# Attention and GLU block on one core: products beside the scores as column tiles, chord additions mostly on GpSimd, chunks of 256 queries, one running-sum bank

## The chip, the cores and the metric

One core of a Trainium2 chip runs the kernel. The metric is the device time of a run in microseconds (us), and lower is better. A run counts as slow when it is over 1.5% above the fastest of its kernel. A page is the profiler's summary of one execution, the span runs from its first to its last instruction, and the granted clock is the share of its full speed that TensorE was allowed. Engine names in the profile are PE (TensorE matrix products), PEld (TensorE weight loads), DVE (VectorE), ACT (ScalarE), POOL (GpSimd) and SP (SyncE, here only transfers).

## The reference, cut to what matters

The input has 2048 rows of 640. There are 32 query heads of size 20, which share one key and one value head. A GELU-gated MLP of width 1536 follows.

```python
def _A_ref(x, wq, wk, wv, wo):
    q = (x @ wq).reshape(B, S, 32, 20).transpose(0, 2, 1, 3)
    k = x @ wk
    v = x @ wv
    scores = jnp.einsum("bhqd,bkd->bhqk", q, k) * (20 ** -0.5)
    p = _softmax(scores, axis=-1)
    o = jnp.einsum("bhqk,bkd->bhqd", p, v)
    return o.transpose(0, 2, 1, 3).reshape(B, S, 640) @ wo

h = x + _A_ref(_layernorm(x), ...)
h2 = h + down(gelu(g) * u)        # g, u: products of layernorm(h) with w_gate, w_up
```

The 32 x 2048 x 2048 exponentials dominate. They are 2048 tiles of 128 keys x 512 columns.

## The kernel before

A score product fills four PSUM banks, one for each 32-row tile of the array. Each bank is a tile of 128x512 scores. ScalarE turns a tile (or two at once) into exponentials in `pa`. VectorE does the same for other tiles by integer arithmetic: it scales a score to the bit pattern of a bf16 power of two, which is a chord of the exponential. Two more copies with 42 and 85 added to the bits give two other chords. The three are summed with different weights in the value product, so a VectorE tile costs one pass over PSUM, two additions in SBUF and three value products instead of one.

```python
CH_SHIFT = (0, 42, 85)
...
# VectorE: the first chord, from PSUM to SBUF as uint16
op = plan.commit("dve", lambda e: e.tensor_scalar(pd[:, 0, s * 512:(s + 1) * 512], bank(b), CH_A, CH_B,
                                                  ALU.mult, ALU.add), c_dve(512), L_DVE, ...)
...
def do_adds(t):                    # VectorE: the other two chords, up to 4 tiles at once
    ...
    for w in (1, 2):
        a = slice(s0 * 512, (s0 + k) * 512)
        op = plan.commit("dve", (lambda w, a: lambda e: e.tensor_scalar(
            pd[:, w, a], pd[:, 0, a], float(CH_SHIFT[w]), None, ALU.add))(w, a), k * 512 / 3.84 + 60.0, L_DVE, ...)
...
# value products: four column tiles of 32, one for each head row
ins = e.matmul(ps[32 * r:32 * r + 32, ab * 512:(ab + 1) * 512], v_ext[:, it["kt"], it["w"], :],
               it["ap"], start=st, stop=(j in ends), tile_position=(0, 32 * r))
```

Every instruction goes through `plan.commit` with an assumed cost in ns. A list scheduler runs once while the program is built. With those costs it fixes the order on each engine, the buffers, and which engine gets which score tile. On the chip the order never changes.

The softmax here doesn't subtract the row's maximum and nothing guards it: scores larger than these inputs give would overflow.

Of the kernel before, what the change touches and what calls it, by code (L numbers as in the profile page):

```python
# [191 lines left out]
def bass_sequential_preLN__grouped_kv_mqa__glu_gated_geglu__prompt_kernel(  # L192
# [30 lines left out]
    CHUNKS = [[0], [1], [2, 3], [4, 5, 6, 7], [8, 9, 10, 11], [12, 13], [14], [15]]  # L223
    BATCHES = [[0, 1, 2, 3], [4, 5, 6, 7], [8, 9, 10, 11], [12, 13], [14], [15]]
    BATCH_COL = [0, 0, 0, 0, 256, 384]
# [65 lines left out]
    def c_mm(n):  # L291
        return max(n / 2.4, 54.0) + 3.0
# [6 lines left out]

    L_PE, L_ACT, L_DVE, L_POOL = 250.0, 165.0, 150.0, 100.0  # L300
# [47 lines left out]
    state = {"mode": "m", "tab": "exp", "npack": 0, "exps_left": 2048, "kv_left": NT, "qk_left": 512}  # L348
# [27 lines left out]
    def ln_group(ln, tiles, prio, done):  # L376
# [27 lines left out]
        def norm(t):  # L404
# [9 lines left out]
            def then(op):  # L414
                s = slot[0]

                def tdone(op2):
                    slots["xt"].append(s)
                    done(t, op2)

                if ln == 0:
                    o = xn1T[:, :, t * P:(t + 1) * P]
                    wkeys = [("xn1T", t)]
                else:
                    o = xn2T[:, :, xcol[t]:xcol[t] + P]
                    wkeys = [("xn2T", xcol[t])]
                sp_tasks.append(_Task(("sp",), lambda e: e.dma_start_transpose(o, xn_tmp[:, s, :]), 1330, 1500,
                                      [("xt", s)], wkeys, prio, tdone))
# [15 lines left out]

    xcol = {}
# [8 lines left out]
    def mm(o, l, r, st, sp, **kw):  # L454
        return lambda e, b: e.matmul(o(b), l, r, start=st, stop=sp, **kw)  # L455
# [95 lines left out]
    def on_job(u, so):  # L551
# [8 lines left out]
        def then(b):  # L560
# [4 lines left out]
            def c1(op):  # L565
# [3 lines left out]
                if nt == 4:  # L569
                    g = gs[0]  # L570
                    o = onq[:, tl[0] % NON:tl[0] % NON + 4, 4 * Dh * g:4 * Dh * (g + 1)].rearrange(
                        "p j (r d) -> p j r d", r=4)
                    parts.append((o, slice(0, 4)))
                elif nt == 2:
                    for gi, g in enumerate(gs):
                        o = onq[:, tl[0] % NON:tl[0] % NON + 2, 4 * Dh * g:4 * Dh * (g + 1)].rearrange(
                            "p j (r d) -> p j r d", r=4)
                        parts.append((o, slice(2 * gi, 2 * gi + 2)))
                else:
                    o = onq[:, tl[0] % NON, 4 * Dh * gs[0]:4 * Dh * (gs[-1] + 1)].rearrange(  # L580
# [10 lines left out]
                for o, js in parts:  # L591
# [4 lines left out]
                        [("onq", t % NON, g) for t in tl for g in (gs if nj == 4 else [gs[js.start // 2]])],  # L596
# [5 lines left out]
        def gate():  # L602
            return bool(slots["rcp"])
# [11 lines left out]
    def on_transpose(t):  # L615
        sl = []
        tk = _Task(("sp",), None, 1330, 1500, [("onq", t % NON, g) for g in range(NG)], [], 1.0, None,
                   lambda: bool(slots["onT"]))

        def bind():  # L620
            s = slots["onT"].pop(0)
            sl.append(s)
            tk.fn = lambda e: e.dma_start_transpose(onT[:, s, :, :], onq[:, t % NON, :])
            tk.writes = [("onT", s)]
# [26 lines left out]
    LN2G = [[0], [1], [2, 3], [4, 5], [6, 7], [8, 9], [10, 11], [12, 13], [14], [15]]  # L651
# [15 lines left out]
    def x2_done(t, op):  # L667
        b = batch_of[t]
        batch_x[b] += 1
        if batch_x[b] == len(BATCHES[b]):  # L670
            for fc in range(NFC):
                gate_job(b, fc)
# [9 lines left out]
    def g_free(b):  # L682

        if b <= 3:
            return all(down_left[x] == 0 for x in range(b))
        return all(down_left[x] == 0 for x in range(min(b, 3)))

    def gu_pieces(w, b, fc):
        n = len(BATCHES[b]) * P
        x0 = xcol[BATCHES[b][0]]  # L690
        return [(mm(lambda bk: bank(bk, n), w[:, c, fc * P:(fc + 1) * P], xn2T[:, c, x0:x0 + n],
                    c == 0, c == NC_D - 1), c_mm(n),
                 [("xn2T", xcol[t]) for t in BATCHES[b]] + ["wg" if w is wg_sb else "wu"]) for c in range(NC_D)]

    def gate_job(b, fc):
        n = len(BATCHES[b]) * P

        def then(bk):
            def fin(op):
                free_bank(bk)  # L700
                gate_left[b] -= 1
# [4 lines left out]
            def fin2(op):  # L706
                free_bank(bk)
                gate_left[b] -= 1
# [3 lines left out]
            o = gbuf[:, fc, gcols(b)]  # L712
            if state["exps_left"] > 0:
                dve(lambda e: e.tensor_copy(o, bank(bk, n)), c_dve(n), [("b", bk)], gkeys(b, fc), 1.0, fin)
            else:
                task(("act",), lambda e: e.activation(o, bank(bk, n), ACT.Gelu_apprx_tanh), ("gelu", c_act(n)), L_ACT,  # L716
                     [("b", bk)], gkeys(b, fc), 1.0, fin2)
        jobs.append(_Job(("gate", b, fc), 5.0, gu_pieces(wg_sb, b, fc), then, lambda: g_free(b)))

    def gelu(b):  # L720
        fcs = sorted(copied[b])
        runs = []
        for fc in fcs:
            if runs and runs[-1][1] == fc and fc - runs[-1][0] < 3:
                runs[-1][1] = fc + 1
            else:
                runs.append([fc, fc + 1])
        n = len(BATCHES[b]) * P
        for f0, f1 in runs:
            v = gbuf[:, f0:f1, gcols(b)]  # L730
            ks = [k for fc in range(f0, f1) for k in gkeys(b, fc)]
            task(("act",), (lambda v: lambda e: e.activation(v, v, ACT.Gelu_apprx_tanh))(v),  # L732
                 ("gelu", c_act(n * (f1 - f0))), L_ACT, ks, ks, 1.0,
                 (lambda f0, f1: lambda op: [up_job(b, fc) for fc in range(f0, f1)])(f0, f1))

    def up_job(b, fc):
        n = len(BATCHES[b]) * P

        def then(bk):
            def fin(op):  # L740
                free_bank(bk)
                up_left[b] -= 1
# [3 lines left out]
            o = gbuf[:, fc, gcols(b)]  # L746
            dve(lambda e: e.tensor_tensor(o, bank(bk, n), o, ALU.mult), c_dve(n), [("b", bk)] + gkeys(b, fc),  # L747
                gkeys(b, fc), 1.0, fin)
# [46 lines left out]


    act_q = []
    dve_q = []
    pend = []
    groups = [(0, 1), (2, 3), (4, 5)]  # L800
# [26 lines left out]
    def free_groups(t):  # L827
        res = []
        for a, b in groups:
            if bank_owner[a] is None and bank_owner[b] is None:  # L830
                r = plan.ready("pe", (), [("b", a), ("b", b)])
                res.append((r, a, b))
        res.sort()
        return [g for g in res if g[0] <= t + 30], res
# [7 lines left out]
    def dve_load(t):  # L842
        v = max(plan.free["dve"] - t, 0.0)
        v += sum(600.0 for x in dve_q) + 300.0 * (len(pend) + len(dve_q))
        m = sum(tk.cost if isinstance(tk.cost, float) or isinstance(tk.cost, int) else 0.0
                for tk in tasks if tk.engs[0] == "dve")
        return v + min(m, 1500.0)

    def issue_qk(t, u, kt, gs):
# [5 lines left out]
        best = None  # L855
        for n, ca in ((0, 1810.0), (1, 1382.0), (2, 904.0), (3, 478.0), (4, 0.0)):
            if n > nf or (n and state["npack"] < 4):
                continue
            m = max(A + ca, Dv + 900.0 * n)
            if best is None or m < best[0] - 1.0:  # L860
                best = (m, n)
        n = best[1]
        (_, a0, a1), (_, b0, b1) = gs[0], gs[1]
# [5 lines left out]
        if n <= 2:  # L869
            lay = [(rr[2], a0), (rr[3], a1), (rr[0], b0), (rr[1], b1)]  # L870
        else:
            lay = [(rr[0], a0), (rr[1], a1), (rr[2], b0), (rr[3], b1)]
# [10 lines left out]
        sw = 0.0 if state["mode"] == "q" else SW  # L883
# [6 lines left out]
        if n == 0:  # L890
            act_q.append(("P", [tiles[rr[0]], tiles[rr[1]]]))
            act_q.append(("P", [tiles[rr[2]], tiles[rr[3]]]))
        elif n == 1:
            dve_q.append(tiles[rr[0]])
            act_q.append(("S", [tiles[rr[1]]]))
            act_q.append(("P", [tiles[rr[2]], tiles[rr[3]]]))
        elif n == 2:
            dve_q.append(tiles[rr[0]])
            dve_q.append(tiles[rr[1]])
            act_q.append(("P", [tiles[rr[2]], tiles[rr[3]]]))  # L900
        else:
            for i in range(n):
                dve_q.append(tiles[rr[i]])
            if n == 3:
                act_q.append(("S", [tiles[rr[3]]]))
# [6 lines left out]
        state["npack"] += 1  # L912
        state["qk_left"] -= 1
# [3 lines left out]
    def acc_bank(u):  # L917
        if u["acc"] is None:
            for b in (6, 7):
# [21 lines left out]
    def issue_pv(t, qs, k):  # L941
# [29 lines left out]
        sw = 0.0 if state["mode"] == "v" else SW  # L971
        state["mode"] = "v"
        op = plan.commit("pe", fn, 216.0 * k + sw, L_PE, reads, writes, at=t)
# [37 lines left out]
    def pe_decide(t):  # L1011
        cand = next_pack(t)
        ok, allg = free_groups(t)
        if cand and len(ok) >= 2:
# [4 lines left out]
        if cand:  # L1019
            est = [g[0] for g in allg]  # L1020
            ta = plan.free["act"]
            fin = {}
            for kind, tl in act_q:
                ta = max(ta, tl[0]["vis"]) + c_act(512 * len(tl))
                for x in tl:
                    fin[x["b"]] = ta + L_ACT
            td = plan.free["dve"]
            for x in dve_q:
                td = max(td, x["vis"]) + 600
                fin[x["b"]] = td + L_DVE  # L1030
            have = set((g[1], g[2]) for g in allg)
            for a, b in groups:
                if (a, b) not in have:
                    e1 = fin.get(a, None)
                    e2 = fin.get(b, None)
                    ra = plan.ready("pe", (), [("b", a), ("b", b)])
                    if (e1 is None and bank_owner[a] is not None) or (e2 is None and bank_owner[b] is not None):
                        est.append(1e12)
                    else:
                        est.append(max(e1 or 0, e2 or 0, ra))  # L1040
            est.sort()
            tq = est[1]
# [6 lines left out]
        press = pa_free.count(True) < 5 or (pd_free.count(True) < 3)  # L1049
        if press and nr == 0:  # L1050
            nr = min(most, 1)
        piece = next_piece(t)

# [3 lines left out]
        def do_pv():  # L1057
            sw = 0.0 if state["mode"] == "v" else SW
            k = int((lim - t - sw) // 216.0) if lim < 1e11 else 3
            k = max(1, min(k, nr, 4))  # L1060
# [8 lines left out]
        swv = 0.0 if state["mode"] == "v" else SW  # L1069
        swm = 0.0 if state["mode"] == "m" else SW  # L1070
        can_v = nr >= 1 and (fits(216.0 + swv) or press)
# [375 lines left out]
```

## Time and profile before

The median is 849.52 us. The profiled run has a span of 851.3 us.

| what (before) | number | where |
|---|---|---|
| ScalarE busy | 763.4 us, 90% | page, part 1 |
| VectorE busy | 742.2 us, 87% | page, part 1 |
| GpSimd busy | 26.9 us, 3% | page, part 1 |
| attention | 24.5 to 792 us | first and last exponential on ScalarE |
| tail | 59.5 us | span less the start of the last exponential (791.8 us) |

First come two parts of the page of the kernel before: busy time by engine with the share of the span and the instruction count, and the shares of the chain that ended last.

```profile
PE 730.3 (86%) x6973; PEld 269.4 (32%) x6973; DVE 742.2 (87%) x1856; ACT 763.4 (90%) x1070; POOL 26.9 (3%) x60
...
ACT 66%; PE 20%; DVE 10%; DMA 3%; issue 1%; SPq 0%; DVEq 0%
```

Next, the costliest groups of the same page. The columns are: line, engine, operation, output from input, shapes and count | busy us, mean ns of one | idle time before, and what ended it. A group whose line says "+1 forms" mixes shapes in its mean.

```profile
L1212 ACT ACTIVATE pa<-ps 128x512 bf16<-128x512 f32 (+1 forms) x1006 | 722.1, 935 | 21.4 <-PE ps L880 20.7
L1263 DVE TENSOR_SCALAR pd<-ps 128x512 uint16<-128x512 f32 x520 | 355.2, 687 | 48.4 <-PE ps L880 40.7
...
L1245 DVE TENSOR_SCALAR pd<-pd 128x512 uint16<-128x512 uint16 (+2 forms) x832 | 230.2, 319 | 8.8
```

Then two windows from the middle of the attention. The columns after the stretch and its length are busy us and instruction count of PE, PEld, DVE, ACT and POOL, then the granted clock, the DMA share and GB/s.

```profile
200.00:400.00 200.00, 176.90 (x1615) 53.99 (x1611) 183.25 (x439) 195.86 (x269) 0.70 (x1) 0.95 0.02 5
400.00:600.00 200.00, 182.25 (x1685) 58.20 (x1683) 187.65 (x450) 198.04 (x274) 1.41 (x2) 0.98 0.06 11
```

ScalarE is 98 to 99% busy there, VectorE 92 to 94%, and GpSimd stands idle. That is why the additions look like work to give away: 230 us of VectorE time.

Only a few GpSimd instructions exist in this kernel. The following are three of its groups with the shapes kept apart, and below them two single instructions of one line (count: duration in ns as min/median/max, first and last start).

```profile
L491 POOL TENSOR_SCALAR v_ext<-v_ext 128x40 bf16<-128x40 bf16 x14 | 4.9, 348 | 22.1 <-DVE v_ext L505 15.5 <-DVE ln_r L397 4.0 <-DVE ln_veb L389 2.0
L332 POOL COPY wq_pad<-gbuf 128x400 bf16<-128x400 bf16 x8 | 3.8, 520 | 4.3 <-DMA gbuf<-in_A_wq_dram 4.3
...
L491 POOL TENSOR_SCALAR v_ext<-v_ext 128x20 bf16<-128x20 bf16 x4 | 1.3, 327 | 0.9 <-ACT v_ext L504 0.7
...
L491 POOL TENSOR_SCALAR v_ext<-v_ext x1: 258/258/258, 25.0 to 25.0; 128x20 bf16<-128x20 bf16 x1
L491 POOL TENSOR_SCALAR v_ext<-v_ext x1: 308/308/308, 29.4 to 29.4; 128x40 bf16<-128x40 bf16 x1
```

A copy of 400 elements takes 0.52 us. The scalar operation that the change wants to send there is present only with 20 and 40 elements.

### The profile page before, as it was taken

What the parts mean: (1) busy time and instruction counts of PE and PEld (TensorE: products, weight loads), DVE (VectorE), ACT (ScalarE), POOL (GpSimd) and SP (SyncE); (2) the same over time, 40 slices, a digit from 0 to 9 for tenths busy, and PEclk for the clock granted to TensorE, in tenths of its full rate; (3) what the DMA queues carried; (4) which work ended last, traced back from release to release, by engine and by line L of the source; (5) the groups of instructions that cost most, each with busy time, mean ns of one, the idle gap of its engine ahead of it and who ended that gap; (6) DMA issues with size and microseconds to landing.
All of it is one profiled execution on the core that took longest, in us unless ns stands there. A gap on an engine that the chain in (4) does not pass through costs nothing.

```text
span 851.3 us, 17702 instructions
## 1 busy us (share of the span) xinstructions
PE 730.3 (86%) x6973; PEld 269.4 (32%) x6973; DVE 742.2 (87%) x1856; ACT 763.4 (90%) x1070; POOL 26.9 (3%) x60
## 2 busy tenths in 40 slices
PE   0877778778889989999998998999999999898998
PEld 0522222222222222233332222223333333232587
DVE  7768988987898989999999998999999999899533
ACT  0779999999999999999999999999999999999322
POOL 5300000000000000000000000000000000000000
PEclk9969979996898999999999998999999999999999
DMA  6780000100000000000021000000102000000100
GB/s 180 144 283 1 16 2 9 10 1 1 7 12 16 1 2 1 2 1 8 27 31 32 2 1 1 2 1 2 39 2 55 2 2 17 17 9 9 32 17 33
DMA packets 42930, 21.84 MB, mean 26 GB/s; under 512 B 34016, under 2 KB 41568, under 8 KB 42848
## 3 DMA queue, kind: packets, MB, share of 16 engines
q1 hardware_dynamic: 40224, 19.83, 9.6%
q8 instruction: 57, 0.93, 0.5%
q10 hardware_dynamic: 2624, 0.87, 0.5%
q14 instruction: 25, 0.20, 0.1%
HBM read 10.21 MB, written 2.62 MB: 15 GB/s over the span
## 4 chain that ended last, share of the span: by engine, by line
ACT 66%; PE 20%; DVE 10%; DMA 3%; issue 1%; SPq 0%; DVEq 0%
ACT pa L1212 64%; PE ps L455 11%; PE ps L968 5%; PE ps L880 5%; DVE pd L1263 4%; DVE pd L1245 2%; ACT gbuf L732 1%; DMA xn1T<-xn_tmp 1%; DMA xh<-in_A_x_dram 1%; DVE stats L374 1%; DVE stats L367 1%; DMA onT<-onq 0%; DVE xn_tmp L435 0%; DVE xh L646 0%; ACT L1212 0%
## 5 line engine op out<-in xcount | busy, mean ns | idle before, releaser
L1212 ACT ACTIVATE pa<-ps 128x512 bf16<-128x512 f32 (+1 forms) x1006 | 722.1, 935 | 21.4 <-PE ps L880 20.7
L1263 DVE TENSOR_SCALAR pd<-ps 128x512 uint16<-128x512 f32 x520 | 355.2, 687 | 48.4 <-PE ps L880 40.7
L968 PE MATMUL ps<-pd,v_ext 128*32 128x512 bf16 x1560 | 280.3, 405 | 21.3 <-ACT pa L1212 14.1
L968 PE MATMUL ps<-pa,v_ext 128*32 128x512 bf16 x1528 | 272.2, 404 | 11.8 <-ACT pa L1212 8.0
L880 PE MATMUL ps<-qT,kT 32*128 32x512 bf16 x2048 | 211.4, 401 | 53.9 <-ACT pa L1212 26.0
L1245 DVE TENSOR_SCALAR pd<-pd 128x512 uint16<-128x512 uint16 (+2 forms) x832 | 230.2, 319 | 8.8
L880 PEld LDWEIGHTS ps<-qT,kT 32*128 32x128 bf16 x2048 | 57.9, 91 | 229.5 <-DVE pd L1263 195.1
L968 PEld LDWEIGHTS ps<-pd,v_ext 128*32 128x32 bf16 x1560 | 67.2, 95 | 110.1 <-issue 47.9
L968 PEld LDWEIGHTS ps<-pa,v_ext 128*32 128x32 bf16 x1528 | 66.1, 94 | 92.4 <-issue 42.0
L455 PE MATMUL ps<-xn2T,wu_sb 128*128 128x512 bf16 (+2 forms) x360 | 69.0, 317 | 6.0 <-DVE gbuf L747 5.9
L455 PE MATMUL ps<-xn2T,wg_sb 128*128 128x512 bf16 (+2 forms) x360 | 68.1, 311 | 0.0
L455 PE MATMUL ps<-xn1T,wq_pad 128*128 128x128 bf16 (+2 forms) x320 | 47.9, 288 | 21.1 <-DMA xn1T<-xn_tmp 20.3
L455 PE MATMUL ps<-wd_sb,gbuf 128*128 128x320 bf16 x384 | 59.6, 300 | 0.0
L747 DVE TENSOR_TENSOR gbuf<-ps,gbuf 128x512 bf16<-128x512 f32 (+2 forms) x72 | 36.5, 509 | 18.3 <-PE ps L455 11.9
L716 ACT ACTIVATE gbuf<-ps 128x128 bf16<-128x128 f32 (+1 forms) x36 | 11.2, 312 | 38.1 <-PE ps L455 38.1
L455 PEld LDWEIGHTS ps<-wd_sb,gbuf 128*128 128x128 bf16 x384 | 34.3, 98 | 20.9 <-issue 8.1
L455 PEld LDWEIGHTS ps<-xn2T,wu_sb 128*128 128x128 bf16 x360 | 26.6, 99 | 32.3 <-issue 14.3
L393 POOL TENSOR_TENSOR ln_denb<-ln_veb,halfc 128x2 bf16<-128x2 bf16 (+1 forms) x19 | 12.6, 673 | 749.1 <-DVE ln_veb L389 749.1
L455 PEld LDWEIGHTS ps<-xn1T,wq_pad 128*128 128x128 bf16 x320 | 23.2, 103 | 39.8 <-DMA xn1T<-xn_tmp 20.3
L455 PEld LDWEIGHTS ps<-xn2T,wg_sb 128*128 128x128 bf16 x360 | 25.8, 98 | 25.1 <-issue 14.7
L766 DVE TENSOR_TENSOR xh<-xh,ps 128x320 bf16<-128x320 bf16 x32 | 15.4, 482 | 17.4 <-PE ps L455 17.4
L455 PE MATMUL ps<-wo_sb,onT 128*128 128x320 bf16 x160 | 28.3, 301 | 0.1
(47 smaller groups left out, 266.2 us busy)
## 6 DMA issues: line engine op xcount, KB each, us to landing
out_dram<-xh SPq DMA_DIRECT2D x16, 160.0 KB, 1.8
xh<-in_A_x_dram SPq DMA_DIRECT2D x3, 640.0 KB, 9.9
wg_sb<-in_B_w_gate_dram SPq DMA_DIRECT2D x1, 1920.0 KB, 8.9
wu_sb<-in_B_w_up_dram SPq DMA_DIRECT2D x1, 1920.0 KB, 10.2
wd_sb<-in_B_w_down_dram SPq DMA_DIRECT2D x1, 1920.0 KB, 14.0
gbuf<-in_A_wq_dram ACTq DMA_DIRECT2D x2, 400.0 KB, 8.3
wo_sb<-in_A_wo_dram SPq DMA_DIRECT2D x1, 800.0 KB, 5.3
xh<-in_A_x_dram SPq DMA_DIRECT2D x2, 160.0 KB, 2.8
```

The source lines that it names most:

```text
L367: dve(lambda e: e.bn_stats(stats[:, ln, t, 6:12], xh[:, t, HALF:D]), 356, [key], [("st", ln, t, 1)], prio, c)
L374: dve(lambda e: e.bn_stats(stats[:, ln, t, 0:6], xh[:, t, 0:HALF]), 356, [key], [("st", ln, t, 0)], prio, b)
L393: task(("pool",), lambda e: e.tensor_tensor(ln_denb[:, ln, sl], ln_veb[:, ln, sl], halfc[:, 0:n], ALU.pow), 1010, L_POOL, [("veb", kk), "h ...
L455: return lambda e, b: e.matmul(o(b), l, r, start=st, stop=sp, **kw)
L716: task(("act",), lambda e: e.activation(o, bank(bk, n), ACT.Gelu_apprx_tanh), ("gelu", c_act(n)), L_ACT, [("b", bk)], gkeys(b, fc), 1.0, fin2)
L747: dve(lambda e: e.tensor_tensor(o, bank(bk, n), o, ALU.mult), c_dve(n), [("b", bk)] + gkeys(b, fc), gkeys(b, fc), 1.0, fin)
L766: dve(lambda e: e.tensor_tensor(xh[:, t, h * HALF:(h + 1) * HALF], xh[:, t, h * HALF:(h + 1) * HALF], bank(bk, HALF), ALU.add), c_dve(HALF ...
L880: ins = e.matmul(bank(b), kT4[32 * r:32 * r + 32, kt * P:(kt + 1) * P], qT[32 * r:32 * r + 32, s, :], start=True, stop=True, tile_position ...
L968: ins = e.matmul(ps[32 * r:32 * r + 32, ab * 512:(ab + 1) * 512], v_ext[:, it["kt"], it["w"], :], it["ap"], start=st, stop=(j in ends), ti ...
L1212: op = plan.commit("act", lambda e: e.activation(dst, src, ACT.Exp, scale=SM_SCALE), cost, L_ACT, [("b", b0 + i) for i in range(n)], [("pa ...
L1245: op = plan.commit("dve", (lambda w, a: lambda e: e.tensor_scalar(pd[:, w, a], pd[:, 0, a], float(CH_SHIFT[w]), None, ALU.add))(w, a), k * ...
L1263: op = plan.commit("dve", lambda e: e.tensor_scalar(pd[:, 0, s * 512:(s + 1) * 512], bank(b), CH_A, CH_B, ALU.mult, ALU.add), c_dve(512), ...
```

## The change

The intent: GpSimd takes most of the additions, so VectorE can take more score tiles from ScalarE. TensorE changes between only two tilings, because all products beside the scores are split in four column tiles like the value products. Chunks of at most 256 queries let the MLP of early rows run inside the attention. With one bank for the running sum, other banks can hold scores. Gate and up products fill a whole bank before they are evicted. The core of the diff (the plumbing of buffers and of the scheduler's choices is left out):

```diff
-    CHUNKS = [[0], [1], [2, 3], [4, 5, 6, 7], [8, 9, 10, 11], [12, 13], [14], [15]]
-    BATCHES = [[0, 1, 2, 3], [4, 5, 6, 7], [8, 9, 10, 11], [12, 13], [14], [15]]
+    CHUNKS = [[0, 1], [2, 3], [4, 5], [6, 7], [8, 9], [10, 11], [12, 13], [14], [15]]
+    BATCHES = CHUNKS
...
+    POOL_ADD = 520.0
+    ADD_MIN = 2
...
+        def fn(e, b, mode):
+            if mode == "m":
+                return e.matmul(o(b), l, r, start=st, stop=sp)
+            ins = None
+            for j in range(4):
+                a = slice(32 * j, 32 * j + 32)
+                ins = e.matmul(o(b)[a, :], l[:, a], r, start=st, stop=sp, tile_position=(0, 32 * j))
+            return ins
...
     def acc_bank(u):
         if u["acc"] is None:
+            if state["kv_left"] == 0 and any(bank_owner[b] is not None and bank_owner[b][0] == "acc" for b in (6, 7)):
+                return False
...
+        a = slice(s0 * 512, (s0 + k) * 512)
+        cost, lat = (k * 512 / 3.84 + 72.0, L_DVE) if eng == "dve" else (POOL_ADD, L_POOL)
+        op = plan.commit(eng, lambda e: e.tensor_scalar(pd[:, w, a], pd[:, 0, a], float(CH_SHIFT[w]), None, ALU.add),
+                         cost, lat, ...)
...
     def pool_decide(t):
...
+        if POOL_ADD:
+            w = 2 if len(pend[2]) >= len(pend[1]) else 1
+            if pend[w] and pend[w][0]["at"] <= t + 20:
+                do_adds(t, "pool", w, 1)
```

The instruction orders of the two programs, which can be compared without a run, show 1146 additions on GpSimd and 119 instructions of addition left on VectorE. VectorE takes 648 score tiles instead of 520. TensorE changes its tiling 1023 times instead of 1272.

## The prediction

> **What bounds the kernel now.** From 24 to 792 us the attention runs, then a tail of about 58 us. The chain of waits gives 64% of the span to the exponentials on ScalarE. The windows of 100 us between 200 and 700 us show ScalarE 98 to 100% busy, VectorE 91 to 96%, TensorE 86 to 92% (its record includes pipeline ends). The groups: 522 pair exponentials (128x1024) and 484 single ones on ScalarE, busy 722.1 us; on VectorE 520 exponentials from the score banks (355.2 us) and 832 chord additions (230.2 us). So ScalarE binds, VectorE is close behind, GpSimd is idle (3%).
>
> **What the change moves** (counts from the two instruction orders):
> 1. VectorE takes 648 of 2048 score tiles, not 520. ScalarE has 389 pairs and 622 singles. In the timeline a pair takes 0.914 us start to start and a single 0.475; both kernels so computed, times 1.02 (what the old sum lacks to 722), give 722 before and 664 after. Six more table loads (1.283 us each) and slightly more GELU work return 10 us. ScalarE: about 48 us less in the attention.
> 2. VectorE loses 713 additions (119 remain, about 38 us; minus 190) and gains 128 tiles (0.60 to 0.65 us start to start; plus 80). Busy falls from 742 to about 635 us.
> 3. GpSimd gets 1146 additions of 128x512 uint16. The case has no such instruction: small GpSimd scalar operations (20 to 40 elements) take 0.26 to 0.31 us, copies of 400 elements come 0.46 us apart. The Trainium skill (GPSIMD Engine Reference, section 3.1) gives 1.03 cycles per element for such bodies, 0.44 us for 512 as an estimate; with overhead I expect 0.52 to 0.7 us, so 600 to 800 us in all. No run here shows it yet. At 0.52 it fits; at 0.65 GpSimd binds beside ScalarE. The same page says (section 8) that contention comes with VectorE's two-port modes or two SBUF inputs; few of those are left, so I expect little.
> 4. TensorE: mode changes fall from 1272 to 1023. The Trainium skill (TensorEngine Tiling, Key Properties) says that a change of mode drains; the timeline agrees, about 0.11 us lost each, so 28 us saved. But four column tiles instead of one instruction nearly double the instructions, small products (128 columns) get slower (estimate 99 instead of 57 ns per group), 256 queries mean more groups, and value products rise from 3088 to 3344 (18 us). Net: TensorE work about 15 to 20 us more, none of it on the path while ScalarE binds.
> 5. Tail: after the last score product some 277 column groups remain (about 28 us), then one tile's projection, norm and GLU (about 28 us): as long as now.
>
> **Sum.** Only the attention shortens: 48 us if ScalarE stays the limit with the same idle time, giving 802. I give back 13 us for idling, as four engines now run at 80 to 95% in a fixed order with one sum bank and freer score banks. Predicted: **815 us**, range 792 to 866 (8 in 10). Faster by over 2%: 0.69; within 2%: 0.16; slower by over 2%: 0.15.
>
> **What would show it.** ScalarE exponentials 655 to 670 us busy and still 94% or more of the attention; VectorE additions below 45 us; GpSimd 600 to 700 us busy with TensorE rarely waiting for its additions; the last exponential ends near 755 us; tail 53 to 60 us.
>
> **What would make it wrong.** A GpSimd addition over 0.65 us: value products then wait for GpSimd, buffers of the VectorE tiles stay full, and the time goes to 850 us or beyond. Column tiles limited by weight loads would make TensorE the limit. Planned order not matching real durations would leave ScalarE idle.

## The result, and the profile after

The changed kernel takes 1776.68 us (median of 2 runs), against 849.52 us. The ratio is 2.091, with a 95% interval of 2.082 to 2.100. Every ratio in this document is the mean time of one kernel's fast runs over that of the other's in the same rounds, so it is not quite the ratio of the medians. The prediction was 815 us, and even its range ended at 866.

The same parts of the page after:

```profile
PE 996.2 (56%) x13866; PEld 385.8 (22%) x13866; DVE 679.3 (38%) x1268; ACT 757.0 (43%) x1055; POOL 1697.3 (96%) x1205
...
POOL 93%; issue 3%; DMA 1%; PE 1%; DVE 1%; SPq 0%; POOLq 0%
```

GpSimd went from 3 to 96% busy and holds 93% of the chain; ScalarE and VectorE stand idle more than half of the time. The groups of the page after:

```profile
L1329 POOL TENSOR_SCALAR pd<-pd 128x512 uint16<-128x512 uint16 x1146 | 1671.6, 1488 | 3.0 <-DVE ln_vb L399 2.2
L1296 ACT ACTIVATE pa<-ps 128x512 bf16<-128x512 f32 (+1 forms) x1011 | 712.6, 762 | 939.3 <-PE ps L988 802.9
L1350 DVE TENSOR_SCALAR pd<-ps 128x512 uint16<-128x512 f32 x648 | 432.2, 687 | 931.4 <-PE ps L988 927.7
L1067 PE MATMUL ps<-pa,v_ext 128*32 128x512 bf16 x1400 | 381.7, 515 | 448.3 <-POOL pd L1329 447.7
```

One addition on GpSimd takes 1.488 us, not 0.52, and GpSimd waited only 3.0 us before all 1146 of them: it never had nothing to do. The sum is the whole time. The first addition starts at 35.7 us. 1146 of them keep GpSimd busy for 1671.6 us, about 11 us go to norms, small copies and idling between them, and the last one starts at 1716.7 us and ends near 1718. With the 35.7 us before the first addition and the 56 us after the last, that is the span of 1774.5 us.

The waits of the same run (engine, line, what it waited for: us in total, times, longest) show how the delay is handed on:

```profile
DVE pd L1350 <- PE ps L988: 927.7, 354, 8.5
PEld ps L1067 <- POOL pd L1329: 834.1, 393, 7.9
ACT pa L1296 <- PE ps L988: 802.9, 348, 10.6
PE ps L1067 <- POOL pd L1329: 697.6, 351, 7.6
```

TensorE waits for GpSimd in the value products (the second and fourth line). The order of its work is fixed, so the next score product stands behind that wait, and ScalarE and VectorE wait for the score product. A stretch of the timeline (start us, us, engine, line, operation, and in brackets the idle time before it) shows one such wait:

```profile
803.96 4.39 POOL L1329 TENSOR_SCALAR pd<-pd 128x512 uint16<-128x512 uint16 x3
...
804.41 0.57 PE L1067 MATMUL ps<-pa,v_ext 128*32 128x512 bf16 x1
804.41 0.57 PE L1067 MATMUL ps<-pd,v_ext 128*32 128x512 bf16 x2
...
806.95 0.39 PE L1067 MATMUL ps<-pd,v_ext 128*32 128x512 bf16 x1 [1.97 <-POOL pd L1329]
```

The three additions take 4.39 us, and between 804.98 and 806.95 us TensorE does nothing.

The granted TensorE clock is 0.70 after and 0.96 before, and a matrix product takes 0.515 us instead of 0.404. The column tiles are not the reason: the second experiment has them too, and its clock is 0.96. The lower clock came together with a TensorE that was idle for 44% of the span; what sets it was not tested. It is not what made the run long either, since GpSimd waited for others for only 3.0 us before its additions.

### The profile page after: what moved, and what is told of

Read it like the earlier page. It is cut to its first block, busy times and chain, and to the rows that moved or that the text cites. A ratio compares the mean times of both kernels' runs of the same rounds, so it can differ in the third digit from the quotient of the medians.

```text
span 1774.5 us, 32037 instructions
## 1 busy us (share of the span) xinstructions
PE 996.2 (56%) x13866; PEld 385.8 (22%) x13866; DVE 679.3 (38%) x1268; ACT 757.0 (43%) x1055; POOL 1697.3 (96%) x1205
## 4 chain that ended last, share of the span: by engine, by line
POOL 93%; issue 3%; DMA 1%; PE 1%; DVE 1%; SPq 0%; POOLq 0%
POOL pd L1329 93%; DMA xn1T<-xn_tmp 1%; PE ps L487 1%; DMA xh<-in_A_x_dram 0%; POOL ln_denb L407 0%; PE ps L491 0%; DVE stats L388 0%; DVE stats L381 0%; POOL v_ext L529 0%; PE ps L1067 0%; DVE pd L1350 0%; DMA xn2T<-xn_tmp 0%; DVE xn_tmp L452 0%; DVE gbuf L809 0%; DVE ln_vb L399 0%
## 5 line engine op out<-in xcount | busy, mean ns | idle before, releaser
L1329 POOL TENSOR_SCALAR pd<-pd 128x512 uint16<-128x512 uint16 x1146 | 1671.6, 1488 | 3.0 <-DVE ln_vb L399 2.2
L1350 DVE TENSOR_SCALAR pd<-ps 128x512 uint16<-128x512 f32 x648 | 432.2, 687 | 931.4 <-PE ps L988 927.7
L1067 PE MATMUL ps<-pa,v_ext 128*32 128x512 bf16 x1400 | 381.7, 515 | 448.3 <-POOL pd L1329 447.7
L1067 PE MATMUL ps<-pd,v_ext 128*32 128x512 bf16 x1944 | 412.3, 518 | 260.8 <-POOL pd L1329 250.0
L491 PE MATMUL ps<-xn2T,wg_sb 128*32 128x256 bf16 (+1 forms) x1920 | 99.5, 362 | 2.2 <-issue 2.0
L491 PE MATMUL ps<-xn2T,wu_sb 128*32 128x256 bf16 (+1 forms) x1920 | 93.1, 349 | 2.5 <-issue 1.5
L491 PE MATMUL ps<-wd_sb,gbuf 128*32 128x320 bf16 x1440 | 77.6, 353 | 1.0 <-issue 1.0
L491 PE MATMUL ps<-xn1T,wq_pad 128*32 128x256 bf16 (+1 forms) x1440 | 71.2, 345 | 0.4 <-DMA xn1T<-xn_tmp 0.4
L491 PEld LDWEIGHTS ps<-xn2T,wu_sb 128*32 128x32 bf16 x1920 | 57.9, 122 | 34.7 <-issue 19.5
L1329 DVE TENSOR_SCALAR pd<-pd 128x512 uint16<-128x512 uint16 (+2 forms) x119 | 62.7, 530 | 0.0
L809 DVE TENSOR_TENSOR gbuf<-ps,gbuf 128x512 bf16<-128x512 f32 x48 | 32.8, 684 | 51.8 <-PE ps L491 41.3
```

Of the source, the lines that this page charges most:

```text
L491: ins = e.matmul(o(b)[a, :], l[:, a], r, start=st, stop=sp, tile_position=(0, 32 * j))
L809: dve(lambda e: e.tensor_tensor(o, i, o, ALU.mult), c_dve(n * k), [("b", bk)] + ks, ks, 1.0, fin)
L1329: op = plan.commit(eng, lambda e: e.tensor_scalar(pd[:, w, a], pd[:, 0, a], float(CH_SHIFT[w]), None, ALU.add), cost, lat, [("pd", 0, s0 + ...
```

## The experiments

The theory after the result (A): the duration of the GpSimd addition is the whole loss. The rivals: (B) the addition is slow only because VectorE and GpSimd contend for SBUF; (C) another part of the change (column tiles, one sum bank, the clock) costs much as well. "Before" in the table is the median of the kernel before in the same rounds.

| label | what | us | before | ratio (95%) |
|---|---|---|---|---|
| e2_no_pool | no addition on GpSimd | 850.30 | 851.76 | 0.9965 (0.991 to 1.002) |
| e3_pool_1480 | planned at 1.48 us | 881.63 | 851.76 | 1.034 (1.028 to 1.040) |
| e4_int32_pool | packed int32 add, old plan | 944.33 | 851.76 | 1.107 (1.101 to 1.113) |
| e5_short_add | 128 of 512 columns (wrong result) | 842.06 | 852.34 | 0.988 (0.984 to 0.992) |
| e6_int32_740 | packed int32, planned at 0.74 | 859.47 | 852.34 | 1.009 (1.005 to 1.013) |
| e7_both_all | both copies in one instruction | 866.58 | 852.34 | 1.016 (1.012 to 1.021) |
| e8_both_mix | the same, VectorE helps | 880.71 | 852.34 | 1.035 (1.031 to 1.039) |
| e9_full_array | e2 without column tiles | 845.26 | 852.13 | 0.992 (0.989 to 0.995) |
| e10_old_chunks | e2 with the old chunks | 866.79 | 852.13 | 1.018 (1.014 to 1.023) |
| e11_short_32 | e5 with 32 columns (wrong result) | 840.20 | 852.13 | 0.986 (0.983 to 0.990) |
| e12_honest | e7 planned at measured costs | 858.38 | 852.13 | 1.007 (1.004 to 1.011) |

All other outputs of the experiments were correct. e1_bench is a single run (862.72 us, state unknown) and serves for durations alone.

### e1_bench: what one GpSimd instruction costs

The kernel before, with forms of instruction on a scratch tile, three each, placed once in the attention and once in the tail:

```diff
+        for rep in range(3):
+            add(lambda e, o: e.tensor_scalar(o[:, 0:512], bin_[:, 0:512], 42.0, None, ALU.add))
+        ...                                  # 256 and 128 columns; bf16 512; f32 256
+            add(lambda e, o: e.tensor_tensor(o[:, 0:512].bitcast(I32), bin_[:, 0:512].bitcast(I32),
+                                             bcon[:, 0:512].bitcast(I32), ALU.add))
+        ...                                  # bf16 512, two inputs; copy of uint16 512
+    bench([("v", 14, 2), ("v", 15, 2)])      # in the attention
+    bench([("lr", (1, 15))])                 # after the last norm
```

> The kernel before, with eight forms of GpSimd instruction on a scratch tile, three of each, once while VectorE works on the attention and once in the tail after the last norm. Theory A (the uint16 scalar add is slow by itself on GpSimd): 128x512 uint16 takes 1.4 to 1.5 us in both places, and 256 and 128 columns fall in proportion to about 0.75 and 0.4 us, 2.5 to 2.9 ns per column. Rival B (contention with VectorE for the SBUF interface): 1.4 us only in the first place and about 0.5 us in the tail. Open: whether the type is to blame; if so, bf16 512 and f32 256 columns take 0.45 to 0.6 and 0.25 to 0.4 us. The two-input int32 add of 256 columns is estimated at 0.55 to 0.8 us.

The groups of GpSimd in the tail of this run, from 805 us on, where VectorE is 43% busy:

```profile
L803 POOL TENSOR_SCALAR bench_out<-bench_in 128x512 uint16<-128x512 uint16 x3 | 4.4, 1496 | 0.9 <-DVE ln_r L400 0.9
L809 POOL TENSOR_SCALAR bench_out<-bench_in 128x512 bf16<-128x512 bf16 x3 | 4.4, 1491 | 0.1
L818 POOL TENSOR_TENSOR bench_out<-bench_in,bench_con 128x512 bf16<-128x512 bf16 x3 | 3.4, 1152 | 0.0
L812 POOL TENSOR_SCALAR bench_out<-bench_in 128x256 f32<-128x256 f32 x3 | 2.5, 850 | 0.0
L805 POOL TENSOR_SCALAR bench_out<-bench_in 128x256 uint16<-128x256 uint16 x3 | 2.5, 850 | 0.0
L815 POOL TENSOR_TENSOR bench_out<-bench_in,bench_con 128x256 int32<-128x256 int32 x3 | 2.1, 724 | 0.0
L821 POOL COPY bench_out<-bench_in 128x512 uint16<-128x512 uint16 x3 | 1.7, 615 | 0.0
L807 POOL TENSOR_SCALAR bench_out<-bench_in 128x128 uint16<-128x128 uint16 x3 | 1.5, 529 | 0.0
```

And the addition over both places (min/median/max in ns):

```profile
L803 POOL TENSOR_SCALAR bench_out<-bench_in x6: 1488/1490/1506, 54.2 to 818.8; 128x512 uint16<-128x512 uint16 x6
```

The addition takes 1.49 us in both places. In the first one VectorE is 93% busy (54 to 75 us) and its own additions of 512 columns take 0.487 us, yet GpSimd's are no longer than in the tail. So rival B is refuted as the cause of the 1.49 us; contention can add something to GpSimd's time, a tenth in the worst group (256 columns of f32: 0.941 us there, 0.850 in the tail). The type does not matter either (1.491 us for a bf16 multiplication). From 256 to 512 columns it grows by 640 ns, which is 2.5 ns a column, with about 0.21 us fixed. That fixed part was not in my expectation for the narrow forms (0.75 and 0.4 us; measured 0.850 and 0.526). The copy takes 0.615 us for the same columns. The surprise is the two-input form: 1.152 us for 512 columns, cheaper than the one with a constant. My guess for packed pairs (0.55 to 0.8 us) held: 0.724 us.

The kernel before already hinted at this. Its two single instructions above take 258 ns for 20 elements and 308 ns for 40. That is 2.5 ns an element and 208 ns fixed, which gives 1.49 us for 512. They were picked after the result was known: all four of 20 elements took 257 to 428 ns, all fourteen of 40 took 307 to 535. The means of the two groups (327 and 348 ns) would have given 0.84 us, too little, but still above the 0.65 us at which the prediction calls itself wrong. I had read them only as "0.26 to 0.31 us".

### e2_no_pool and e3_pool_1480: without GpSimd, and with the true cost

```diff
-    POOL_ADD = 520.0
-    ADD_MIN = 2
+    POOL_ADD = 0          # e2; e3: POOL_ADD = 1480.0 and ADD_MIN = 2
+    ADD_MIN = 1
```

> The changed kernel planned anew with every chord addition on VectorE, everything else of the change kept. Theory A (GpSimd additions alone cause the loss): 820 to 860 us, near the kernel before, GpSimd about 3% busy. Rival C (column tiles, one sum bank or the lower TensorE clock cause a large part): 1000 us or more.

> The changed kernel planned anew with a GpSimd addition costed at 1.48 us as measured, instead of 0.52: GpSimd gets about 480 additions, VectorE the rest. Theory A: 820 to 860 us, GpSimd about 710 us busy. Rival B/C (contention or column tiles): above 950 us, with VectorE additions far over 0.29 us each.

Without additions on GpSimd the changed kernel takes 850.3 us, the same as before. The loss of 926 us is gone, so rival C is refuted: the rest of the change, taken together, costs nothing measurable. It gains nothing either.

The run planned at 1.48 us missed my range by 22 us, and it is 31 us slower than the one without GpSimd. The two groups of VectorE additions of 512 columns tell part of the reason. First without GpSimd:

```profile
L1329 DVE TENSOR_SCALAR pd<-pd 128x512 uint16<-128x512 uint16 x558 | 138.5, 284 | 1.7
```

And beside 478 GpSimd additions:

```profile
L1329 DVE TENSOR_SCALAR pd<-pd 128x512 uint16<-128x512 uint16 x192 | 77.5, 407 | 0.0
```

VectorE is as busy as without the help (757.0 against 755.0 us), although GpSimd makes 478 of the additions. Part of that is 24 more score tiles (591 instead of 567). Most of the rest is that the additions that stayed take longer, 0.407 us instead of 0.284. So B is right about VectorE where it was wrong about GpSimd. This fits the contention that the Trainium skill names (GPSIMD Engine Reference, section 8: the SBUF interfaces are shared, and VectorE instructions in a two-port mode contend); that these additions run in such a mode is not shown by a trace. VectorE's reads from PSUM do not suffer: 0.686 and 0.682 us. That the contention accounts for the whole 31 us is argued, not shown.

### e4_int32_pool, e6_int32_740: a faster form of the same addition

Two 16-bit values are added as one 32-bit integer; neither half overflows. The constant comes from a tile.

```diff
+            fn = lambda e: e.tensor_tensor(pd[:, w, a].bitcast(I32), pd[:, 0, a].bitcast(I32),
+                                           shc[:, w - 1, :].bitcast(I32), ALU.add)      # on GpSimd only
-    POOL_ADD = 520.0
+    POOL_ADD = 740.0         # e6 alone; e4 keeps 520.0
```

> The changed kernel, its plan with 0.52 us per GpSimd addition, but the addition as a two-input int32 add of 256 packed pairs with a constant tile. If this form takes under 0.6 us: 800 to 830 us and the prediction's mechanism holds. If it takes 0.8 us, about 980 us; if 1.4 us, again about 1750 us. The output shows whether the packed add is exact.

> The packed int32 add, now planned at its measured 0.74 us, so that VectorE keeps about a quarter of the additions. If duration alone counts: 815 to 845 us. If the SBUF contention that slowed VectorE additions to 0.85 us beside two-input GpSimd adds counts too: 850 to 900 us.

Both outputs pass the check, as they should if the packed add is exact, which the Trainium skill says (GPSIMD Engine Reference, section 4.1, "Exact integer add"); the check goes by a relative error, so it is no test of single bits. With the plan for 0.52 us the kernel needs 944 us: 1147 additions at 0.735 us keep GpSimd busy for 799 us, more than the whole attention before (767 us). The group of VectorE additions in that run:

```profile
L1334 DVE TENSOR_SCALAR pd<-pd 128x512 uint16<-128x512 uint16 x91 | 77.2, 848 | 0.0
```

They take 0.848 us, three times the 0.284 us without GpSimd. In e6, beside the same form but with GpSimd about 86% busy between 200 and 600 us instead of 95%, they take 0.430 us. Planned at its true cost the form gives 859.5 us, near the lower end of the range I gave for contention. The form is better than the one in the change, and still slower than no GpSimd at all.

### e5_short_add and e11_short_32: if the addition had cost what the plan assumed

The same plan as the change, but the GpSimd addition covers only some columns. The rest stays zero, so the result is wrong.

```diff
+        c = slice(s0 * 512, s0 * 512 + 128) if eng == "pool" else a       # e11: 32
-        op = plan.commit(eng, lambda e: e.tensor_scalar(pd[:, w, a], pd[:, 0, a], float(CH_SHIFT[w]), None, ALU.add),
+        op = plan.commit(eng, lambda e: e.tensor_scalar(pd[:, w, c], pd[:, 0, c], float(CH_SHIFT[w]), None, ALU.add),
```

> The changed kernel with its own plan, but each GpSimd addition covers only 128 of the 512 columns (result wrong on purpose; the buffers are zeroed once, about 4 us at the start). The measuring run gave 0.526 us for this width, the cost that the plan assumed for 512. Theory A (the duration of this one instruction is the whole loss): 800 to 840 us, ScalarE 655 to 670 us busy on exponentials, as predicted blind. Rival (the plan is also wrong elsewhere, for instance in column tiles or contention): above 860 us.

> The same instruction order as the run with 128-column GpSimd additions, but 32 columns each (result wrong on purpose; about 0.29 us by the measured 206 ns plus 2.5 ns per column). If GpSimd still held something up at 0.53 us: under 832 us. If what is left lies in ScalarE and the fixed order: 836 to 846 us.

The groups of e5:

```profile
L1298 ACT ACTIVATE pa<-ps 128x512 bf16<-128x512 f32 (+1 forms) x1014 | 677.1, 796 | 37.6 <-PE ps L990 25.4
L1332 POOL TENSOR_SCALAR pd<-pd 128x128 uint16<-128x128 uint16 x1148 | 587.8, 534 | 138.9 <-DVE pd L1353 125.3
```

And its windows:

```profile
200.00:400.00 200.00, 182.10 (x3430) 83.08 (x3431) 168.88 (x322) 195.30 (x286) 165.04 (x322) 0.98 0.06 12
400.00:600.00 200.00, 181.26 (x3440) 82.87 (x3428) 166.65 (x314) 195.38 (x290) 165.36 (x322) 0.99 0.08 14
```

With an addition of 0.534 us the time falls from 1777 to 842 us. The columns are the only difference beside the zeroing at the start and a plan that shifts a little with it, so the duration of this one instruction is shown to be the cause. (What a long addition does to VectorE goes with it: beside the short ones VectorE's additions of 512 columns take 0.304 us, in the changed kernel 0.479.) At 0.294 us (e11) it is 840 us: the intervals overlap, and GpSimd no longer matters. What is left is ScalarE at 98%. **Even with the cost that was hoped for, the change would have gained 1.2%, not 4%.** I had expected 800 to 840 us, and the upper end was missed by 2 us.

### e7_both_all, e8_both_mix, e12_honest: one instruction for both copies

```diff
+                    op = plan.commit("pool", lambda e: e.tensor_tensor(
+                        pd[:, 1:3, a].bitcast(I32),
+                        pd[:, 0, a].bitcast(I32).unsqueeze(1).to_broadcast([P, 2, 256]),
+                        shc[:].bitcast(I32), ALU.add), POOL_ADD, L_POOL, ...)
# e7: POOL_ADD 1170, VectorE adds only when 5 wait (none do); e8: when 2 wait
# e12: POOL_ADD 1250, when 3 wait; VectorE additions planned 0.28 us longer (as in e7),
#      and each waiting one counted as 150 ns of VectorE's load instead of 50 (ADDW)
```

> One GpSimd instruction makes both shifted copies of a tile (2x256 int32 columns, in0 repeated, estimated at 1.15 to 1.2 us from the 1.152 us of the 512-column two-input form), and VectorE makes none, so there is nothing left to contend with. If the estimate and the theory hold: 805 to 840 us, better than both kernels, GpSimd about 730 us busy. If repeating in0 costs extra (over 1.3 us): over 880 us.

> As the run before it, but VectorE may take additions when two or more wait, about a fifth of them. If contention does no harm: equal to or up to 10 us faster than all on GpSimd. If it does: VectorE additions 0.6 to 0.9 us each and 10 to 50 us slower.

> One GpSimd instruction for both copies of a tile, planned at the measured 1.25 us, and VectorE additions planned 0.28 us longer, as contention makes them. Expected 843 to 860 us: GpSimd near 97% in the attention and ScalarE with fewer stalls than in the run planned at 1.17 us (867 us). A clear gain over the kernel before would need under 835 us.

e7 missed on the slow side (its range ended at 840 us). The GpSimd group of e7:

```profile
L1432 POOL TENSOR_TENSOR pd<-pd,shc 128x512 int32<-128x512 int32 x606 | 747.0, 1291 | 17.1 <-DVE pd L1354 15.1
```

One instruction takes 1.291 us (747.0 / 606 = 1.233 us apart), more than my 1.15 to 1.2, and GpSimd is 98% busy between 200 and 600 us, so it probably binds again. Where VectorE helps (e8), its additions of 512 columns take 0.581 us and the time is 14 us worse, inside the 10 to 50 us of the contention hypothesis; the plan, which put these additions at 0.2 us, is another possible reason. With the measured costs in the plan (e12) it is 858.4 us, inside the range that I gave and no gain; GpSimd is 89 to 93% busy there, not the 97% that I expected.

### e9_full_array and e10_old_chunks: the other parts, one at a time

Both start from the run without GpSimd additions.

```diff
-        md = "m" if state["qk_left"] == 0 and not open_units() else "v"
+        md = "m"                                                   # e9
-    CHUNKS = [[0, 1], [2, 3], [4, 5], [6, 7], [8, 9], [10, 11], [12, 13], [14], [15]]
+    CHUNKS = [[0], [1], [2, 3], [4, 5, 6, 7], [8, 9, 10, 11], [12, 13], [14], [15]]      # e10, batches as before
```

> The run without GpSimd additions, but products beside the scores on the whole array again, as in the kernel before: mode changes rise from 1021 to 1325 in the instruction order, about 0.11 us each, 33 us of TensorE time. If TensorE were on the path: about 870 to 885 us. If the sum of ScalarE and VectorE work binds, as I now think: within 1% of the run without GpSimd additions (843 to 859 us).

> The run without GpSimd additions, with the chunks and batches of the kernel before (up to 512 queries). If the new chunks do nothing for the time: 843 to 859 us. If they pay (earlier GLU work, so less left for the tail): 862 to 880 us, the tail after the last exponential 10 us or more longer.

Without column tiles TensorE changes its tiling 1325 times instead of 1021, and the time is 845.3 us, if anything less. The Trainium skill (TensorEngine Tiling, Key Properties) says that a change of mode drains the array, and the timeline before agrees: 0.32 to 0.33 us pass from a score product to the next product after a change, where rounds of value products without a change come 0.22 us apart, so about 0.11 us are lost. At that rate the 304 changes are worth about 33 us of TensorE time. But the exchange also takes away nearly half of the products (7451 instead of 13704), and TensorE's busy time is 9 us higher (714.5 against 705.9), so this run does not weigh the changes alone. The chunks are another matter. With the old ones, 74 us pass from the start of the last exponential (788.1) to the end (862.3), against 62 us with the new ones (787.1 to 849.3). The smaller chunks save 12 us of tail in this schedule; the other few us of the difference were not followed up. It depends on the schedule: the kernel before has the old chunks and a tail of 59.5 us. The single sum bank and the whole-bank evictions were not tested alone.

The run without GpSimd and without column tiles is the fastest correct version: 845.3 against 852.1 us, 0.8% below the kernel before. That is clear of the noise of these rounds, and below the 2% that a verdict "faster" asks for.

## Why the prediction was wrong, point by point

1. *ScalarE's exponentials, 655 to 670 us busy.* Nearly right where it could be tested: 677.1 us in e5, without the table loads, which are a group of their own. That is 7 us above the range. The fall is 45 us, and 58 were forecast (722 to 664). In the changed kernel itself ScalarE was idle for more than half of the time, so the term had no effect.
2. *VectorE's busy time falls to about 635 us; additions below 45 us.* In e5 it is 640.4 us, with 41.3 us for additions: right. In the changed kernel it is 679.3 us, of which the additions take 62.7, as those of 512 columns take 0.479 us beside GpSimd's long ones instead of 0.304 us.
3. **The step that failed: "with overhead I expect 0.52 to 0.7 us, so 600 to 800 us in all."** It measured 1.488 us each and 1671.6 us in all. The figure came from the Trainium skill (GPSIMD Engine Reference, section 3.1: 1.03 cycles per element for a body of at most two operations) and from a copy in the trace. The measured slope of 2.5 ns is 3 cycles at that page's 1.2 GHz. The same paragraph of the page also has about 1.8 cycles per element as the best case of a tight loop, 769 ns for 512 elements, which the prediction leaves out; that figure alone is above its 0.65 us. The copy is another instruction, with another slope. The mechanism that the prediction named for its own failure ("a GpSimd addition over 0.65 us: value products then wait for GpSimd") is what happened; only the size was far off. A range up to 866 us was too narrow for a cost that I had called unmeasured: 1146 times each 0.1 us is 115 us of GpSimd time.
4. *TensorE's work is 15 to 20 us more, and not on the path while ScalarE binds.* The first half is wrong by the traces: TensorE is busy for 704.3 us in e5 and was for 730.3 before. Small products did not get slower: in e5, 62 products of 128 columns start within 0.85 us (796.78 to 797.63), about 55 ns for each four. The second half was not tested by itself; taking the column tiles back changed little (e9).
5. *The tail stays as long as now, 53 to 60 us.* It grew: 65 us in e5 from the start of the last exponential (771.6) to the end, 59.5 before.
6. *"802, and I give back 13 us for idling".* This would have failed too. The attention shortened by 21 us in e5 (from 767 to 746, first to last start of an exponential), not by 35. ScalarE's whole busy time fell by 42 us, but its idle time before exponentials rose from 21.4 to 37.6, and the tail grew by 5. The gain was overrated even without the error in point 3: 842 us, not 815.

## What to carry to other kernels

Before work is moved to an engine, find the cost of that very instruction at two sizes and extrapolate by slope and fixed part (tiny ones give no more than a hint: here 0.84 or 1.49 us, depending on which are taken). Here a copy on the same engine (0.615 us) said nothing about the addition (1.490 us). Where a fixed plan is made from assumed costs, multiply an unmeasured cost by its count first: that product, not the share of idle time, decides whether the move can work. And an idle engine is not free help: here VectorE's additions took 43 to 199% longer beside GpSimd's full-width ones (0.407 to 0.848 us by the run, instead of 0.284).

## What the Trainium skill lacked or had wrong

- GPSIMD Engine Reference, sections 3.1 and 4.1: a body of at most two operations at 1.03 cycles per element, "1-input is roughly line-rate". A GpSimd scalar add or multiply took about 0.21 us plus 2.5 ns per column (0.526, 0.850 and 1.490 us for 128, 256 and 512), 3 cycles at 1.2 GHz, in uint16, bf16 and f32 alike.
- Section 3.1 of the same page has about 2.6 cycles per element for two inputs. The two-input add took 1.152 us for 512 bf16 columns, 2.7 cycles per column at 1.2 GHz with the fixed part in it, which agrees, and 0.724 us for 256 int32 columns. No page says that the form with a constant is the slower one: 1.490 us for 512 columns.
- Section 8 names the contention with VectorE's two-port modes and gives no size there; another page, SBUF — State Buffer, says more of it, which this document did not use. A VectorE addition of 512 uint16 columns took 0.284 us on average without GpSimd additions, 0.407 and 0.479 us beside scalar adds (e3, the change) and 0.430, 0.581 and 0.848 us beside two-input adds (e6, e8, e4); VectorE instructions that read PSUM stayed at 0.68 to 0.69 us.
- Section 4.1, exact int32 add: no time is given there, and it took 0.735 us for 256 columns in the kernel.
